# Mask-row copies and casts on more engines, with a new order of the work behind batch 0

## The chip, the cores and the metric

The kernel runs on one core of a Trainium2 chip. The core has engines that each execute their own queue of instructions in order: TensorE (PE, with the loading of its weights shown as PEld), VectorE (DVE), ScalarE (ACT), GpSimd (POOL) and SyncE (SP), which here only issues DMA transfers. An instruction whose input is not ready waits, and everything behind it in the same queue waits with it. The metric is the device time of one execution in microseconds (us); smaller is better.

## The reference

Sparse attention is followed by a two-layer network. There are 4 batches, 8 heads, 768 positions and 64 dimensions a head. The keys of a head form 12 blocks of 64. A query's gate scores are its products with the mean key of each block; blocks that lie wholly after the query's own are excluded. A query may attend to the three blocks with the largest scores and to its own block, causally.

```python
k_rep = k.reshape(B, H, n_blocks, block, D).mean(axis=3)
gate_scores = np.einsum('bhsd,bhnd->bhsn', q, k_rep)
gate_scores = np.where(causal, gate_scores, -1000000000.0)
top_idx = np.argsort(gate_scores, axis=-1)[..., -top_k:]
...
scores = np.where(mask, scale * q @ k.T, -1000000000.0)   # mask: chosen blocks and causal
attn_out = softmax(scores) @ v
x = attn_out.transpose(0, 2, 1, 3).reshape(3072, 512)
out = gelu_tanh(x @ w_in) @ w_out          # w_in 512x2048, w_out 2048x512
```

(The last lines are shortened; the softmax is that of each row.)

## The kernel before

**Units.** The heads of a batch are taken two at a time, which gives 16 pairs: pair p belongs to batch p // 4. In the texts, pair 6 is the third pair of batch 1. The network is computed batch by batch as soon as a batch's four pairs are done, so that attention of batch b + 1 runs beside the network of batch b on the same engines.

**Preparing a pair** (`pre(p)`). For pairs from 4 on, queries and keys are loaded by SP in blocks of 32 (line L400, four DMAs for each of q and k) and transposed on DVE (L564). DVE sums the key blocks (L621) and builds the gate's operand (L638). Casts to 16 bits put the transposed keys into `kT` (`kc_all`, one cast for each head) and the queries into `qT` (`q16`, one for each head). The gate is a group of small matmuls (L687). DVE transposes its result (L703), adds the causal part (L710), finds the largest values (L719, ten MAX8), compares (L720) and writes the additive mask `madd` (L724). The mask has 12 rows for each head, one for each key block, once it is turned: they become rows 64 to 76 of `qT`, so that one matmul over 76 rows gives score plus mask. For pairs 4 to 7 the turning is done on PE (L756) and the result lies in PSUM; for pairs 8 to 15 it is a DMA transpose issued by SP (L763) into a tile `mT` in SBUF. From there `mc` copies the 12x640 rows of each head into `qT`. All casts and copies whose engine can be chosen go through `copy` (L361 to L367): L363 is ACT, L365 POOL, L367 DVE.

**Heads** (`heads(p)`). Each head has three groups. A group is a set of score matmuls (L1046) into one of two "wide" PSUM buffers, the exponential on ACT (L1059), a causal select on POOL (L1073), and the matmuls with the values (L1085). DVE divides by the row sums (L968, L969), and the result is turned for the network, on PE (L988) or by a DMA transpose (L993).

**The network.** `s1` is x @ w_in (L1122) with gelu on ACT (L1134). For batch 0 the second product is plain (L1322). For batches 1 to 3 it is computed with seven products of half-size blocks in place of eight (L1372); DVE makes the sums of blocks that this needs (L1309) and joins the results (L1421), and `a_e` copies one part. Batch 3 uses the same trick for the first product (`s1_seven`: L1211, DVE additions at L1170). Filler matmuls (L1524), whose results are not used, stand at some places of PE's queue.

**What sets the order.** The program first records 1,900-odd operations, each with the engines that it may run on and an estimated cost for each. The order of issue, the choice of buffers and the engines were found by a planner beforehand and stand in the file as three tables: `ORDER` (L21, operation numbers), `BUFFER` (L157, buffer picks in that order) and `ENGINE` (L183, operations that don't run on the first engine of their list). `Plan.run` replays them:

```python
for n in ORDER:
    op = self.ops[n]
    for kind, key in op.takes:
        if key not in self.buf:
            self.buf[key] = self.kinds[kind][0][next(picks)]
    op.emit(engine.get(n, next(iter(op.engines))))
```

Each engine gets its operations in the sequence in which they stand in `ORDER`; semaphores between engines are placed by the framework. The cost figures in the calls of `add` are not used when the kernel runs: they are what the planner reckoned with, and their keys are the engines that it could choose.

Of the kernel before, what the change touches and what calls it, by code (L numbers as in the profile page):

```python
# [189 lines left out]
    "POOL": [  # L190
        586, 587, 646, 647, 707, 972, 973, 1035, 1036, 1097, 1098,
        1159, 1160, 1425, 1489, 1551, 1612]}


class Op:
# [40 lines left out]
def kernel(  # L236
# [121 lines left out]
    add = plan.add  # L358
# [169 lines left out]
    def pre(p):  # L528
# [238 lines left out]
        if first:  # L767
            mcs = []
# [858 lines left out]
```

## Time and profile before

| | us |
|---|---|
| median of 3 runs | 257.55 (257.46 to 257.74) |
| the profiled execution | 257.76 |
| span of its instructions | 256.0 |
| PE busy | 246.5 (96%) |
| DVE busy | 191.4 (75%) |
| ACT busy | 176.4 (69%) |
| POOL busy | 84.3 (33%) |
| mean clock that PE was granted | 1.0 of full speed |

The profiled execution is 1.76 us longer than the span, and 0.21 us above the median. Shares are those of the span. In the rows, "L1059 ACT ACTIVATE ats<-wide 128x896 x72 | 63.4, 915 | 8.9 <-PE" reads: line, engine, operation, output from input, shape, count; busy us in total and mean ns of one; idle us of the engine just before them and what ended most of it. A row of a timeline begins with the start and the duration in us, and ends, where the engine sat idle before, with the idle time and its releaser. A row of a table by stretch has for each engine its busy us (and its number of instructions), then the clock, the share of DMA and GB/s. `SPq` are DMA issues in SP's queue.

### The profile page before, as it was taken

How to read it: one execution, taken by the hardware profiler on the slowest of the kernel's cores; microseconds unless marked ns; L12 is line 12 of the kernel's file. 1: busy time of each engine (PE TensorE's matmuls, PEld its weight loads, DVE VectorE, ACT ScalarE, POOL GpSimd, SP SyncE). 2: the span in 40 equal slices, each digit the busy share in tenths (PEclk: the TensorE clock that was granted, in tenths of full speed). 3: DMA queues.
4: the chain of work that ended last, by engine and by line, in shares of the span. 5: the costliest groups of instructions: out<-in, count | busy, mean ns of one | idle time of the engine just before them, and what ended most of it. 6: DMA issues, size and time to landing. Idle time of an engine off the chain costs nothing.

```text
span 256.0 us, 6451 instructions
## 1 busy us (share of the span) xinstructions
PE 246.5 (96%) x2485; PEld 171.2 (67%) x2485; DVE 191.4 (75%) x539; ACT 176.4 (69%) x225; POOL 84.3 (33%) x163
## 2 busy tenths in 40 slices
PE   7889999999998999999899999999999999999994
PEld 5667686555554566555578888555777786766883
DVE  2769751041989889989999999699889665579954
ACT  2399997634898998667969884566889957557300
POOL 8465970000239366223053853100056620000000
PEclk9999999999999999999999999999999999999999
DMA  8997599999989995999899699532112520040024
GB/s 164 218 208 166 94 212 191 213 161 157 184 142 165 153 143 99 172 179 199 127 174 110 144 188 166 118 94 69 26 34 72 64 74 1 3 165 0 3 82 164
DMA packets 130927, 32.62 MB, mean 127 GB/s; under 512 B 124528, under 2 KB 126928, under 8 KB 130896
## 3 DMA queue, kind: packets, MB, share of 16 engines
q1 hardware_dynamic: 126160, 27.62, 65.4%
q0 software_dynamic: 3136, 4.19, 9.7%
q10 hardware_dynamic: 1600, 0.39, 0.8%
q8 instruction: 19, 0.31, 0.5%
q14 instruction: 12, 0.10, 0.1%
HBM read 27.26 MB, written 6.29 MB: 131 GB/s over the span
## 4 chain that ended last, share of the span: by engine, by line
PE 51%; DVE 16%; SPq 11%; DMA 10%; POOL 4%; issue 3%; ACT 3%; ACTq 1%; DVEq 0%; POOLq 0%
PE bank L1372 17%; PE wide L1122 10%; SPq L400 9%; PE wide L1046 6%; PE wide L1211 5%; DMA w_in<-in_moe_w_in_dram 5%; PE bank L1085 5%; PE bank L1322 3%; DVE qT L367 3%; DMA sd<-in_k_dram 3%; DVE sel L719 2%; DVE s L564 2%; DVE XS L1309 2%; DMA G<-in_q_dram 2%; ACT ats L882 1%
## 5 line engine op out<-in xcount | busy, mean ns | idle before, releaser
L1122 PE MATMUL wide<-xT,w_in 128*128 128x384 f16 x416 | 72.6, 326 | 0.0
L1059 ACT ACTIVATE ats<-wide 128x896 f16<-128x896 f32 x72 | 63.4, 915 | 8.9 <-PE wide L1046 6.2
L1134 ACT ACTIVATE G<-wide 128x768 f16<-128x768 f32 x52 | 42.1, 810 | 27.3 <-PE wide L1122 27.0
L1122 PEld LDWEIGHTS <-w_in 128*128 128x128 f16 x416 | 40.0, 98 | 26.8 <-issue 1.3
L1073 POOL TENSOR_SCALAR_AFFINE_SELECT ats<-ats 128x256 f16<-128x256 f16 x72 | 33.3, 475 | 60.3 <-ACT ats L1059 60.2
L1046 PE MATMUL wide<-qT,kT 76*128 76x512 f16 (+3 forms) x192 | 39.1, 305 | 0.1
L564 DVE STREAM_TRANSPOSE s<-sd 128x768 f32<-128x768 f32 x24 | 23.1, 968 | 18.7 <-DMA sd<-in_k_dram 17.2
L1372 PE MATMUL bank<-w_out,G 128*128 128x256 f16 x216 | 31.4, 272 | 0.0
L1372 PEld LDWEIGHTS <-G 128*128 128x128 f16 x288 | 26.9, 98 | 6.0 <-issue 0.3
L1322 PE MATMUL bank<-w_out,G 128*128 128x512 f16 x96 | 28.1, 379 | 0.0
L365 POOL CAST kT<-s 64x768 f16<-64x768 f32 x17 | 15.2, 891 | 37.5 <-DVE s L564 37.0
L1421 DVE TENSOR_TENSOR osb<-bank,osb 128x512 f32<-128x512 f32 (+1 forms) x38 | 22.1, 592 | 5.1 <-PE bank L1372 4.5
L1085 PEld LDWEIGHTS <-ats 128*128 128x128 f16 x504 | 22.2, 98 | 3.9 <-POOL ats L1073 0.4
L1085 PE MATMUL bank<-v,ats 128*128 128x65 f16 x504 | 24.4, 194 | 0.2 <-POOL ats L1073 0.2
L1046 PEld LDWEIGHTS <-kT 76*128 76x128 f16 x192 | 17.3, 98 | 10.5 <-issue 0.8
L1372 PEld LDWEIGHTS <-XS 128*128 128x128 f16 x216 | 20.0, 98 | 5.5 <-DVE XS L1309 1.5
L1372 PE MATMUL bank<-TS,XS 128*128 128x256 f16 x144 | 22.0, 272 | 0.8 <-DVE XS L1309 0.7
L882 ACT ACTIVATE ats<-wide 128x1024 f16<-128x1024 f32 (+3 forms) x24 | 20.8, 924 | 1.3 <-PE wide L863 0.8
L365 POOL CAST v<-vsd 128x768 f16<-128x768 f32 x13 | 11.4, 875 | 13.8 <-DMA vsd<-in_v_dram 8.8
L969 DVE TENSOR_TENSOR xn<-bank,zr 128x384 f16<-128x384 f32 x24 | 13.4, 558 | 0.8
L719 DVE MAX8 sel<-sel 128x8 f32<-128x12 f32 x160 | 13.2, 158 | 0.6
L1322 PEld LDWEIGHTS <-G 128*128 128x128 f16 x96 | 8.9, 98 | 6.1 <-issue 0.3
(120 smaller groups left out, 358.6 us busy)
## 6 DMA issues: line engine op xcount, KB each, us to landing
out_dram<-osb SPq DMA_DIRECT2D x23, 256.0 KB
vsd<-in_v_dram SPq DMA_DIRECT2D x26, 192.0 KB
sd<-in_k_dram SPq DMA_DIRECT2D x48, 96.0 KB
sd<-in_q_dram SPq DMA_DIRECT2D x48, 96.0 KB
w_in<-in_moe_w_in_dram POOLq DMA_DIRECT2D x2, 1024.0 KB, 11.5
w_out<-in_moe_w_out_dram POOLq DMA_DIRECT2D x2, 1024.0 KB, 14.5
G<-in_k_dram SPq DMA_DIRECT2D x4, 192.0 KB
G<-in_q_dram SPq DMA_DIRECT2D x4, 192.0 KB
```

The source lines that it names most:

```text
L365: nc.gpsimd.tensor_copy(out=out, in_=in_)
L400: nc.sync.dma_start(out=T[key, p][64 * hh + 32 * a:64 * hh + 32 * a + 32], in_=SRC[key][b, 2 * hp + hh].rearrange("(t i) (a j) -> a i t j" ...
L564: nc.vector.transpose(out=T[key + "T32", p], in_=T[key, p].rearrange("p t j -> p (t j)"))
L882: nc.scalar.activation(out=T["at", u][:, :, 0:n], in_=plan.buf[("st",) + u].rearrange("p (h w) -> p h w", h=2)[:, :, 0:n], func=AF.Exp, bi ...
L1046: nc.tensor.matmul(st[:, x:e], kT16[i][h][0:76, s0:s0 + 128], qT16[i][h][0:76, s0 + (x - cb):s0 + (e - cb)], start=True, stop=True)
L1059: nc.scalar.activation(out=T["at", u][:, 0:n], in_=plan.buf[("st",) + u][:, 0:n], func=AF.Exp, bias=0.0, scale=SCALE)
L1073: nc.gpsimd.affine_select(out=dg, in_=dg, compare_op=ALU.is_ge, fill=0.0, base=0, pattern=[[0, 2], [1, 128]], channel_multiplier=-1)
L1085: nc.tensor.matmul(pvv[:, qc, 0:65], at[:, cb + (qc - jc) * 128: cb + (qc - jc + 1) * 128], v16[i][:, jc, h, :], start=(gi == 0 and jc == ...
L1122: nc.tensor.matmul(hps[:, 512 * e:512 * e + HALF], w_in16[:, ci, (2 * j + e) * 128: (2 * j + e + 1) * 128], T["xT", b][:, ci, HALF * h:HAL ...
L1134: nc.scalar.activation(out=G[:, :, h, j, :], in_=plan.buf["hps", b, j, h].rearrange("p (e w) -> p e w", e=2)[:, :, 0:HALF], func=AF.Gelu_a ...
L1322: nc.tensor.matmul(plan.buf["ops", b, ti], G[:, f % 2, 2 * ti // NC, f // 2, ti % (NC // 2) * 128:ti % (NC // 2) * 128 + 128], w_out16[:, ...
L1372: nc.tensor.matmul(dst[:, HD * h:HD * h + HD], FACT[m][0][:, j, t * 128:(t + 1) * 128], FACT[m][1][:, j, :], start=(clear and j == 0), sto ...
```

## The change

Four entries of the planner's tables are widened or revised, and the three recorded tables are replaced by the ones that a further search gave.

```diff
-            kcs = [add({DVE: 0.56, POOL: 0.85}, kc_all(h),
+            kcs = [add({DVE: 0.56, POOL: 0.85, ACT: 0.84}, kc_all(h),
...
-            q16s = [add({DVE: 0.56, ACT: 0.84}, q16(h), qcs + [old.get("s")],
+            q16s = [add({DVE: 0.56, ACT: 0.84, POOL: 0.85}, q16(h), qcs + [old.get("s")],
...
-                m = add({"DMA": 0.8}, lambda _: None, [go], pr, lag=6.0)
+                m = add({"DMA": 0.8}, lambda _: None, [go], pr, lag=3.5)
...
-            mcs = [add({DVE: 0.5, ACT: 0.7} if byPE else {DVE: 0.33}, mc(h),
+            mcs = [add({DVE: 0.5, ACT: 0.7} if byPE else
+                       {DVE: 0.4, POOL: 0.72, ACT: 0.66}, mc(h),
...
 ENGINE = {
     "ACT": [
         67, 72, 74, 85, 90, 94, 101, 110, 114, 121, 130, 134, 141,
-        329, 331, 345, 346, 348, 449, 467, 486, 504, 523, 541, 580,
-        595, 597, 628, 657, 658, 718, 893, 929, 980, 981, 1043, 1044,
-        1106, 1167, 1202, 1434, 1559, 1668, 1674, 1677, 1698, 1704,
-        1707, 1727, 1736, 1786, 1822],
+        329, 331, 348, 349, 449, 467, 486, 504, 523, 541, 580, 587,
+        597, 598, 628, 657, 857, 893, 929, 972, 973, 985, 1035, 1036,
+        1047, 1048, 1167, 1172, 1202, 1425, 1438, 1489, 1550, 1668,
+        1674, 1677, 1698, 1704, 1707, 1727, 1733, 1736, 1786, 1822],
     "POOL": [
-        586, 587, 646, 647, 707, 972, 973, 1035, 1036, 1097, 1098,
-        1159, 1160, 1425, 1489, 1551, 1612]}
+        345, 346, 586, 646, 647, 655, 707, 708, 716, 984, 1097, 1098,
+        1106, 1159, 1160, 1168, 1171, 1426, 1437, 1496, 1500, 1501,
+        1551, 1562, 1563, 1612, 1613, 1624, 1625]}
```

The mask-row copies from `mT` could only run on DVE before and may run on three engines now. The first 346 entries of `ORDER`, with all of batch 0's attention, are the same. Behind them `ORDER` and `BUFFER` differ throughout (some 100 lines of numbers, left out here). Eight filler matmuls (operations 1921 to 1928) are no longer in `ORDER`: three stood near 63 us of the profiled execution, one near 70 us, and four between 230 and 235 us.

Forty-five operations run on another engine:

| from, to | what |
|---|---|
| DVE to ACT (10) | mask rows from PSUM of pairs 4 and 5 (349, 598); mask rows from `mT` of pairs 8, 9, 11 and 12 (985, 1047, 1048, 1172, 1438); a key cast of pair 14 (1550); one `a_e` copy (857) and one copy of 128x768 in `s1_seven` (1733) |
| DVE to POOL (16) | mask rows from `mT` of pairs 8 and 11 to 15 (984, 1171, 1437, 1500, 1501, 1562, 1563, 1624, 1625); seven casts of pairs 6, 7, 11, 12, 13 and 15 (655, 708, 716, 1168, 1426, 1496, 1613) |
| ACT to DVE (9) | mask rows from PSUM of pairs 6 and 7 (658, 718); seven query casts of pairs 5, 8, 9, 12 and 14 (595, 980, 981, 1043, 1044, 1434, 1559) |
| ACT to POOL (3) | query casts of pairs 4 and 10 (345, 346, 1106) |
| POOL to ACT (7) | key casts of pairs 5, 8, 9, 12 and 13 (587, 972, 973, 1035, 1036, 1425, 1489) |

Among the other moves in `ORDER`, the gates of pairs 14 and 15 stand some 6 us of PE work earlier, and SP's DMA issues from pair 12 on stand in another sequence. What is computed is the same.

255 rows, old and new, of tables (BUFFER, ORDER) are left out of this document.

## The prediction

> **What bounds the kernel now.** I read the page's busy line and chain first, then TensorE's waits, then its idle time by stretch, and last the other engines there.
>
> ```profile
> PE 246.5 (96%) x2485; PEld 171.2 (67%) x2485; DVE 191.4 (75%) x539; ACT 176.4 (69%) x225; POOL 84.3 (33%) x163
> PE 51%; DVE 16%; SPq 11%; DMA 10%; POOL 4%; issue 3%; ACT 3%; ACTq 1%; DVEq 0%; POOLq 0%
> ...
> PE bank L756 <- DVE madd L724: 1.2, 1, 1.2
> PE bank L1372 <- DVE XS L1309: 0.7, 1, 0.7
> PE bank L1085 <- POOL ats L1073: 0.2, 1, 0.2
> ```
>
> TensorE (PE) is busy for 246.5 of 256.0 us, so other engines count only where they make it wait. The last three rows are its waits from 61 us on, where the two orders part (columns: us, times, longest). The same shows by stretch:
>
> ```profile
> core 0: us, PE busy (x) PEld busy (x) DVE busy (x) ACT busy (x) POOL busy (x), PEclk, DMA share, GB/s
> 75.00:85.00 10.00, 8.80 (x91) 5.24 (x88) 9.68 (x27) 8.77 (x12) 8.58 (x15) 1.00 1.06 161
> 85.00:97.00 12.00, 11.96 (x149) 7.33 (x147) 10.38 (x32) 10.71 (x15) 5.78 (x12) 1.00 0.92 126
> 97.00:110.00 13.00, 13.00 (x131) 8.07 (x129) 12.53 (x43) 10.25 (x13) 4.87 (x7) 1.00 1.04 145
> 122.00:135.00 13.00, 12.07 (x121) 8.88 (x119) 12.69 (x46) 10.08 (x14) 4.18 (x8) 1.00 1.13 147
> 185.00:205.00 20.00, 19.76 (x252) 15.34 (x250) 16.25 (x33) 17.89 (x21) 13.16 (x25) 1.00 0.32 54
> ...
> 61.00:140.00 79.00, 76.84 (x720) 47.62 (x719) 70.85 (x206) 63.01 (x81) 31.91 (x53) 1.00 1.07 156
> 140.00:205.00 65.00, 64.76 (x698) 47.74 (x696) 56.85 (x153) 49.94 (x62) 24.85 (x46) 1.00 0.56 96
> ```
>
> Between 61 and 205 us PE lacks 79.00 − 76.84 + 65.00 − 64.76 = 2.4 us. Half of it lies at 75 to 85 (1.20) and most of the rest at 122 to 135 (0.93), in both of which VectorE (DVE) is full: 9.68 of 10 and 12.69 of 13 us. Of DVE's slack, then, the change can sell at most about 2.4 us of PE time. ACT at 17.89 of 20 in the last heads, and DVE at 12.53 of 13 at 97 to 110, are full without costing PE anything: they are where a new wait would come from.
>
> **The change, part by part.** The first 346 entries of the order are the same, to about 61 us; so what is lost before that stays.
>
> *Fillers.* Eight filler matmuls (L1524) go: three near 63 us, one near 70, four between 230 and 235.
>
> ```profile
> 230.43 0.38 PE L1372 MATMUL bank<-w_out,G 128*128 128x256 f16 x2
> 230.65 0.27 PE L1524 MATMUL bank<-XS 128*128 128x256 f16 x1
> 230.76 0.81 PE L1211 MATMUL wide<-sd 128*128 128x384 f16 x4
> ```
>
> From a filler's start to the next matmul's is 0.11 us, so eight hold 0.88. No wait stands beside them; if they only filled time in which PE would have waited, they return 0. I take −0.7, nearer to the rows.
>
> *Who does the copies.* Forty-five copies and casts change engine: from DVE ten go to ACT and sixteen to GpSimd (POOL); ACT gives nine to DVE and three to POOL; POOL gives seven key casts to ACT. Their prices:
>
> ```profile
> L367 DVE COPY qT<-mT 12x640 f16<-12x640 f16 x16 | 7.1, 445 | 0.4
> L367 DVE CAST qT<-s 64x768 f16<-64x768 f32 x13 | 8.6, 660 | 0.2
> L363 ACT CAST qT<-s 64x768 f16<-64x768 f32 x11 | 9.1, 827 | 0.2
> L363 ACT COPY qT<-bank 12x640 f16<-12x640 f16 x5 | 3.4, 680 | 1.8 <-PE bank L756 0.9 <-DVE qT L367 0.8
> L365 POOL CAST kT<-s 64x768 f16<-64x768 f32 x17 | 15.2, 891 | 37.5 <-DVE s L564 37.0
> L510 POOL MEMSET madd<- 128x640 f16 x4 | 2.6, 644 | 0.0
> L367 DVE COPY qT<-bank 12x640 f16<-12x640 f16 x3 | 1.5, 488 | 0.7 <-ACT qT L363 0.7
> L367 DVE COPY osb<-bank 128x256 f32<-128x256 f32 x5 | 2.1, 419 | 2.6 <-PE bank L1372 2.6
> L367 DVE COPY ats<-wide 128x768 f32<-128x768 f32 x1 | 1.0, 958 | 0.1
> L363 ACT COPY ats<-wide 128x768 f32<-128x768 f32 x5 | 4.0, 799 | 3.1 <-PE wide L1211 3.1
> L1059 ACT ACTIVATE ats<-wide 128x896 f16<-128x896 f32 x72 | 63.4, 915 | 8.9 <-PE wide L1046 6.2
> ```
>
> DVE loses fourteen of its sixteen copies of turned mask rows (14 × 0.445 = 6.2), eight casts (8 × 0.66 = 5.3) and two evictions (0.42 + 0.96), and takes seven casts (4.6): about −8.3 us. ACT takes eight casts (6.6), five mask copies (5 × 0.68 = 3.4) and the two evictions (0.80, and some 0.4 for the smaller), and gives ten casts (8.3): about +2.9, two PSUM mask copies each way cancelling. POOL takes nine mask copies and ten casts and gives seven casts: 3 × 0.89 + 9 × a price the trace does not show. A copy of 12x640 lies between 0.445 (DVE's row) and 0.89 (POOL's larger cast); I take 0.65, the MEMSET with the same 640 columns: 5.9, so +8.5. None of this is on the path by itself; what counts is the wait that it ends or makes.
>
> *The wait at 81.74.*
>
> ```profile
> 76.79 1.78 DVE L367 CAST qT<-s 64x768 f16<-64x768 f32 x2
> ...
> 79.37 0.82 DVE L719 MAX8 sel<-sel 128x8 f32<-128x12 f32 x10
> 80.22 1.06 DVE L720 TENSOR_TENSOR sel<-sel,sel 128x120 f32<-128x120 f32 x1
> ...
> 81.74 0.45 PE L756 MATMUL bank<-ident,madd 128*128 128x128 f16 x5 [1.20 <-DVE madd L724]
> ```
>
> PE waits 1.20 us for pair 6's selection. Ahead of it in DVE's queue two mask copies from PSUM now go to ACT (2 × 0.49, DVE's price for that form) and one of the two casts at 76.79 to POOL (half of 1.78); one cast comes in (0.66). That is 0.98 + 0.89 − 0.66 = 1.2 us earlier, with the mask matmul at its old place in PE's order. Between 0 (POOL's cast stands in DVE's way) and −1.2, I take −1.0.
>
> *The wait at 126.71.* Here DVE does two selections in a row and then the sums (L1309) that the halves at L1372 need. In the new order the four copies of turned mask rows of pairs 8 and 9 leave DVE (1.8 us), against one cast more (0.66): the sums come about 1.1 us earlier, more than the 0.72 that PE waited. I take −0.7, and 0 as the other end. The 0.2 behind the selects (L1073) goes with the new order of the last heads: −0.2 to 0, taken −0.2.
>
> *What is late next: ACT.* Behind each moved copy on ACT stand exps of 0.915 us, and PE's second matmuls (L1085) stand behind those through POOL's select. From 85 to 97 ACT has 10.71 of 12 us; in the new order about one mask copy or cast of 0.7 to 0.83 more stands there, and from 117 to 130 the three copies on ACT wait for a DMA transpose first. I put 0 to 0.8 on each place; by the durations the first is the likelier to be late: +0.5 and +0.3.
>
> *What is late next: DVE at 97 to 122.* Two query casts of pairs 8 and 9 come from ACT into the stretch that begins with 12.53 of 13 us, 2 × 0.66 = 1.3 us, ahead of transposes, selections and the gate of pair 11. The work in DVE's queue from pair 9's query transpose to that gate, each instruction by its duration in this trace, sums to 18.8 to 19.7 us, and the new order has 18.8 us of PE work beside it: 0 to +1.0, taken +0.3.
>
> *The gates of pairs 14 and 15, moved.* They stood here:
>
> ```profile
> 166.96 0.94 DVE L564 STREAM_TRANSPOSE s<-sd 128x768 f32<-128x768 f32 x1
> ...
> 153.61 1.64 SPq L993 DMA_TRANSPOSE xT<-xn  x1
> 158.36 4.08 SPq L400 DMA_DIRECT2D sd<-in_q_dram  x4
> 167.80 0.75 PE L687 MATMUL bank<-s,ksb 128*32 128x160 f32 x16
> ```
>
> The same pair of gates now comes some 6 us of PE work earlier, and PE executes in order: whatever is behind them waits too. Pair 15's query load (four DMAs, 4.08 us of SP's queue) stands behind the DMA transposes of the outputs of pairs 8, 9 and 10 (the last issued at 153.61), as before, and DVE's transpose (0.94) behind the load. In SP's new queue its key load and the value load of pair 13 are ahead of these transposes (3.0 us) and others behind (some 2.9), so that the load comes only 1 to 3 us earlier; its transpose then ends at 164 to 167 less the slack of 2 to 4 us that DVE had ahead of it, 162 to 164, and PE comes to the gates at about 163: 0 to +1.0, taken +0.3.
>
> *The mask copies in ACT's and POOL's queues.* Now an in-order queue with exps or selects behind waits for a DMA transpose.
>
> ```profile
> L763 SPq DMA_TRANSPOSE mT<-madd x8: 1200/1238/2685, 106.6 to 182.8; - x8
> L367 DVE COPY qT<-mT x16: 317/319/939, 120.0 to 193.1; 12x640 f16<-12x640 f16 x16
> ```
>
> The first copy started 13.4 us after the first issue and the last ones 10.3 us after the last, so the rows do not show how short the lag may be; if it is below the planner's new 3.5 plus 0.8, no copy of the new order comes early by my walk through it. 0 to +1.5 for the worst single hold; taken +0.1, near the lower end, since the rows' lags are long. Sundry small waits of a new order that I can't place: +0.2.
>
> *Sum* against the profiled execution, 257.76 us (span 256.0 and 1.76 around it): −0.7 − 1.0 − 0.7 − 0.2 + 0.5 + 0.3 + 0.3 + 0.3 + 0.1 + 0.2 = −0.9. The additions are taken at a third to two thirds of their upper ends, since the walk found little slack there but no certain wait. The profiled execution stands 0.21 above the median of 257.55, so that the median of the changed kernel is put at 257.55 − 0.9 = 256.65, rounded 256.6.
>
> **A page's rule against it.** In the rows above, the compare at 80.22 (L720) took 1.06 us; the one at 72.43 took 0.28.
>
> ```profile
> 72.43 0.28 DVE L720 TENSOR_TENSOR sel<-sel,sel 128x120 f32<-128x120 f32 x1
> 80.33 0.82 POOL L365 CAST v<-vsd 128x768 f16<-128x768 f32 x1
> ```
>
> A POOL cast of 0.82 ran over it, and the excess is 0.78: DVE stood still for it. The Trainium skill, "SBUF — State Buffer", section "Who interferes with whom", says that a DVE instruction with two SBUF inputs, or a copy or cast in a two-port mode, and a GpSimd instruction that reads SBUF share one port pair, an exclusive lock: the second fully blocks until the first ends. The trace agrees with it in this row. By that rule each of the 19 operations that POOL takes could hold DVE for its whole length, where a sum without it lets both run side by side (−0.9); what that would come to is the first rival.
>
> **Rivals.**
> *POOL holds DVE (slower).* Place: the query cast of pair 6 and two casts of pair 7 on POOL between 77 and 97 us, a mask copy at 120 to 122. For: the row at 80.22, and a full DVE there. Against: POOL takes what DVE no longer does, and from 160 to 185 PE works on long matmuls without need of DVE. Price: the 1.0 at 81.74 isn't gained, and three locks of 0.78 (2.3) reach PE: −0.9 + 1.0 + 2.3 = +2.4, 259.9. It decides from two locks that reach PE on (1.6 against the gain of 0.9).
> *A queue held by a mask copy (slower).* ACT or POOL waits for the DMA transpose with three exps behind: one hold of 1.5 and the gates' 1.0 in place of the taken 0.1 and 0.3: −0.9 + 1.4 + 0.7 = +1.2, 258.8. It decides from a hold of about 1.0 on. For: 14 of 16 such copies leave DVE; against: 10 to 13 us of lag in the rows.
> *It does nothing that can be measured.* PE's waits only move: fillers return 0.4, and what the ended waits give the new ones take: 257.0 to 258.0, with 257.2 by these numbers. The three runs spread over 0.28 us, so 0.2% (0.5 us) is about what a measurement of this kernel can tell from no change.
> *Nearly all waits go.* −0.88 for the fillers, −2.1 for the three waits, and none new: 254.6, the floor, since PE's own work is unchanged.
>
> **How the numbers follow.** Forecast (255.5 to 257.0) 0.40; nearly all gone 0.10; nothing measurable 0.14; POOL holds DVE 0.20; a queue held 0.16. So faster 0.50, same 0.14, slower 0.36. The range leaves out half of the floor case and about a tenth above: 255.0 to 260.8; the likeliest case alone has 255.5 to 257.0. An order with so many hands changed has small waits that no walk by hand finds, and that is why slower keeps more than a third.
>
> **What would show it.** Right: PE's wait of 1.2 us for the selection at L724 is gone, that of 0.7 for L1309 too, PE busy near 245.7, idle from 61 to 205 us near 1.5, DVE busy down by 5 to 9 us, POOL up by some 8. Wrong: a wait of PE for L703 or L564 at the moved gates, for L1059 or L1073 at the second matmuls, compares and casts on DVE of 0.8 us or more beside POOL's new copies, or copies of `mT` on ACT or POOL that end a long idle time of their engine with a DMA named as the cause. The prediction falls if PE's idle time from 61 to 205 us is over 2.9 us, which uses up what the fillers give.

## The result, and the profile after

The changed kernel takes 260.91 us (260.81 to 261.02, 4 runs) where the kernel before takes 257.61 us beside it: a ratio of 1.0128, with a 95% interval of 1.0111 to 1.0146. It is 3.3 us slower. The profiled execution has a span of 259.1 us, 3.1 more than before. First the page's busy line of the changed kernel, then its waits of PE from 61 us on (us, times, longest), then PE's table by stretch.

```profile
PE 246.5 (95%) x2477; PEld 171.0 (66%) x2477; DVE 186.5 (72%) x522; ACT 179.5 (69%) x230; POOL 93.6 (36%) x175
...
PE bank L1086 <- POOL ats L1074: 1.9, 2, 1.6
PE wide L1123 <- DMA xT<-xn: 1.8, 1, 1.8
PE wide L1047 <- ACT ats L1060: 1.1, 1, 1.1
PE bank L756 <- DVE madd L724: 0.7, 2, 0.4
PE bank L687 <- DVE s L564: 0.7, 1, 0.7
...
61.00:140.00 79.00, 77.20 (x734) 48.37 (x733) 69.96 (x203) 65.03 (x84) 31.71 (x55) 1.00 0.97 151
140.00:205.00 65.00, 60.82 (x643) 44.29 (x641) 51.08 (x135) 48.62 (x60) 29.85 (x51) 1.00 0.61 101
```

(Line numbers behind about 800 are one higher than before; in the experiments' rows they are three or four lower, since their tables are set in fewer lines.) ACT has 3.1 us more and POOL 9.3 more, about as reckoned (2.9 and 8.5); DVE has only 4.9 less, where 8.3 were reckoned. From 61 to 140 us PE's idle time fell from 2.16 to 1.80 us. From 140 to 205 us, where it had been 0.24, it is now 65.00 − 60.82 = 4.18. So the loss was made in a part of the kernel that had none to lose, and three waits carry it: for the outputs' DMA transpose (1.8), at the moved gates (0.7) and for a causal select (1.6). In the earlier stretch the waits at 81.74 and 126.71 are gone, and three others, of 1.06, 0.39 and 0.34 us, stand there.

### The profile page after: what moved, and what is told of

Same layout as the page of the kernel before. It is cut to its first block, busy times and chain, and to the rows that moved or that the text cites. A ratio compares the mean times of both kernels' runs of the same rounds, so it can differ in the third digit from the quotient of the medians.

```text
span 259.1 us, 6443 instructions
## 1 busy us (share of the span) xinstructions
PE 246.5 (95%) x2477; PEld 171.0 (66%) x2477; DVE 186.5 (72%) x522; ACT 179.5 (69%) x230; POOL 93.6 (36%) x175
## 4 chain that ended last, share of the span: by engine, by line
PE 73%; DVE 9%; ACT 6%; POOL 4%; DMA 3%; issue 2%; SPq 2%; DVEq 0%; POOLq 0%; ACTq 0%
PE wide L1123 24%; PE bank L1373 16%; PE wide L1047 7%; PE bank L1323 6%; PE wide L1212 5%; PE bank L1086 5%; ACT ats L1060 2%; PE wide L864 2%; PE bank L932 2%; POOL ats L1074 2%; PE bank L1525 2%; PE bank L687 2%; ACT ats L883 2%; DMA sd<-in_q_dram 1%; SPq L400 1%
## 5 line engine op out<-in xcount | busy, mean ns | idle before, releaser
L1123 PE MATMUL wide<-xT,w_in 128*128 128x384 f16 x416 | 73.4, 326 | 1.9 <-DMA xT<-xn 1.8
L1135 ACT ACTIVATE G<-wide 128x768 f16<-128x768 f32 x52 | 42.1, 811 | 28.6 <-PE wide L1123 28.0
L1074 POOL TENSOR_SCALAR_AFFINE_SELECT ats<-ats 128x256 f16<-128x256 f16 x72 | 32.0, 458 | 50.1 <-ACT ats L1060 49.3
L1373 PE MATMUL bank<-w_out,G 128*128 128x256 f16 x216 | 33.9, 272 | 0.0
L1373 PEld LDWEIGHTS <-G 128*128 128x128 f16 x288 | 26.9, 98 | 6.0 <-issue 0.3
L1373 PE MATMUL bank<-TS,XS 128*128 128x256 f16 x144 | 22.8, 272 | 0.1
L365 POOL CAST qT<-s 64x768 f16<-64x768 f32 x7 | 6.4, 922 | 21.3 <-DVE ksb L638 21.0
L365 POOL COPY qT<-mT 12x640 f16<-12x640 f16 x9 | 7.8, 871 | 14.4 <-DMA mT<-madd 14.0
```

The source lines that it names most:

```text
L365: nc.gpsimd.tensor_copy(out=out, in_=in_)
L1074: nc.gpsimd.affine_select(out=dg, in_=dg, compare_op=ALU.is_ge, fill=0.0, base=0, pattern=[[0, 2], [1, 128]], channel_multiplier=-1)
L1123: nc.tensor.matmul(hps[:, 512 * e:512 * e + HALF], w_in16[:, ci, (2 * j + e) * 128: (2 * j + e + 1) * 128], T["xT", b][:, ci, HALF * h:HAL ...
L1135: nc.scalar.activation(out=G[:, :, h, j, :], in_=plan.buf["hps", b, j, h].rearrange("p (e w) -> p e w", e=2)[:, :, 0:HALF], func=AF.Gelu_a ...
L1373: nc.tensor.matmul(dst[:, HD * h:HD * h + HD], FACT[m][0][:, j, t * 128:(t + 1) * 128], FACT[m][1][:, j, :], start=(clear and j == 0), sto ...
```

## The experiments

**Four mask copies back on DVE.** The wait of 1.6 us for a select lies at 192 us, in the last heads. POOL's timeline of the changed kernel there (start, us):

```profile
186.75 0.92 POOL L365 COPY qT<-mT 12x640 f16<-12x640 f16 x1
187.72 1.05 POOL L365 CAST kT<-s 64x768 f16<-64x768 f32 x1
188.84 0.61 POOL L1074 TENSOR_SCALAR_AFFINE_SELECT ats<-ats 128x256 f16<-128x256 f16 x1
189.51 1.32 POOL L365 COPY qT<-mT 12x640 f16<-12x640 f16 x1
190.90 1.28 POOL L1074 TENSOR_SCALAR_AFFINE_SELECT ats<-ats 128x256 f16<-128x256 f16 x2
...
192.24 0.61 PE L1086 MATMUL bank<-v,ats 128*128 128x65 f16 x14 [1.58 <-POOL ats L1074]
```

POOL works here without a pause, and two mask copies stand between the selects. The first experiment moves only the engines:

```diff
 # ENGINE["POOL"] of the changed kernel: mask copies of pairs 14 and 15
-        1551, 1562, 1563, 1612, 1613, 1624, 1625
+        1551, 1612, 1613
```

> The changed kernel with only the four turned-mask copies of pairs 14 and 15 back on DVE (from POOL); order as changed. Theory A (POOL's queue): these copies, 0.8 to 1.3 us each on POOL, stand between the causal selects of the last heads, and PE's 1.6 us wait for a select at 192 us comes from them; the wait falls below 0.4 and the time by 1.2 to 1.7 us, to 259.2 to 259.7. Theory B (the new order is tight everywhere): the wait moves to exps or selects next to it, gain under 0.5, 260.4 or more.

Measured: 260.09 us, ratio to the kernel before 1.0095 (1.0082 to 1.0108), which is 0.8 us better than the changed kernel and lies between the times of the two theories. The wait is gone as theory A has it, but not all of its time came back:

```profile
PE wide L1119 <- DMA xT<-xn: 2.5, 2, 1.7
PE bank L1082 <- POOL ats L1070: 0.3, 1, 0.3
```

PE's waits for a select fell from 1.9 to 0.3; in this execution those for `xT`, which lie ahead of the edit, were longer by 0.7. Since PE's order is that of the changed kernel, the start of the same matmul can be compared in the two traces: PE is 0.6 us later than there at 159.47, 1.2 earlier behind the select (192.24), and 0.7 earlier from 195.4 on, behind a new wait for a normalization on DVE. So the copies on POOL made that wait; the gain in time, 0.8, is below the 1.2 that was expected.

**One key load behind a DMA transpose.** The wait for `xT` is a wait for DMA transposes which SP issues. SP's timeline of the changed kernel:

```profile
151.60 1.26 SPq L994 DMA_TRANSPOSE xT<-xn  x1
152.92 1.71 SPq L400 DMA_DIRECT2D sd<-in_k_dram  x3
154.74 1.21 SPq L994 DMA_TRANSPOSE xT<-xn  x1
156.04 2.20 SPq L394 DMA_DIRECT2D vsd<-in_v_dram  x2
158.29 4.45 SPq L400 DMA_DIRECT2D sd<-in_q_dram  x7
...
159.47 0.48 PE L1123 MATMUL wide<-xT,w_in 128*128 128x384 f16 x2 [1.84 <-DMA xT<-xn]
```

Three DMAs of pair 15's key load go out at 152.92, and the transpose of pair 10's output only behind them.

```diff
 # ORDER, SP's operations only
-    1597, 1015, 918, 1077, 1598, 1139, 1543, 1544, 1540, 1601, 1602
+    1597, 1015, 918, 1077, 1139, 1598, 1543, 1544, 1540, 1601, 1602
```

> The changed kernel with one entry of the order moved: the last three DMAs of pair 15's key load are issued behind the DMA transpose of pair 10's output instead of ahead of it in SP's queue. Theory A (SP's queue): the transpose is issued some 1.7 us earlier, PE's wait of 1.8 us for xT at 159 us falls to 0 to 0.4, time 259.0 to 259.6. Theory B: the transpose lands late because the DMA engines are shared with the loads, or the pair 15 gate becomes late by the same amount; gain under 0.6, 260.3 or more.

Measured: 260.78 us, ratio 1.0135 (1.0112 to 1.0158): no gain. Four of the six runs lie at 260.39 to 260.88, the other two at 262.14 and 262.26. PE's wait for `xT` in this run, and the gates of pairs 14 and 15, first in the changed kernel and then here:

```profile
PE wide L1119 <- DMA xT<-xn: 0.5, 1, 0.5
...
167.15 0.75 PE L687 MATMUL bank<-s,ksb 128*32 128x160 f32 x16 [0.66 <-DVE s L564]
...
166.75 0.75 PE L683 MATMUL bank<-s,ksb 128*32 128x160 f32 x16 [1.92 <-DVE s L560]
```

The wait at 159.47 is gone, as theory A has it (the 0.5 that is left belongs to another transpose, at 154.75), and the wait at the gates rose from 0.7 to 1.9, so that the outcome is that of theory B. But the gates did not become later: they start 0.4 us earlier than in the changed kernel. The query loads are issued 0.3 us later than there (158.56 against 158.29), which is next to nothing, and PE simply comes sooner to gates that wait for them. The wait for `xT` had covered most of this second wait.

**The rest of SP's queue.** The value load of pair 14, whose matmuls come some 30 us later, stood ahead of the query loads of pairs 14 and 15. It is moved behind them, and the whole key load of pair 15 behind the transpose.

```diff
 # ORDER, SP's operations only
-    1597, 1015, 918, 1077, 1598, 1139, 1543, 1544, 1540, 1601, 1602
+    1015, 918, 1077, 1139, 1597, 1598, 1540, 1601, 1602, 1543, 1544
```

> The changed kernel with only SP's queue re-sequenced between 145 and 163 us: all four DMAs of pair 15's key load behind the DMA transpose of pair 10's output, and the value load of pair 14 behind the query loads of pairs 14 and 15. Theory A (what stands ahead in SP's queue makes both waits): PE's wait for xT (1.8 us) and its wait at the moved gates (0.7 us; 1.9 us where only the key load was moved) are both below 0.4; time 258.3 to 259.1. Theory B (the DMA engines are the limit, so one of the two is late whatever the sequence): the sum of both stays above 1.5 us, 260.1 or more.

Measured: 258.63 us, ratio 1.0037 (1.0024 to 1.0050). The time is that of theory A, 2.3 us less than the changed kernel, but by waits it is only half right. No wait for `xT` is left. The wait at the gates, which theory A had below 0.4, is longer than in the changed kernel, 1.5 against 0.7, and the sum of both stands at the bound that theory B gave. Some 1.0 of the gain comes from waits for a select, which fell from 1.9 to 0.9 without an edit there; the second mask copy took 0.92 us on POOL here and not 1.32, and what made it shorter was not tested.

```profile
164.75 0.98 DVE L560 STREAM_TRANSPOSE s<-sd 128x768 f32<-128x768 f32 x1 [0.80 <-DMA sd<-in_q_dram]
...
165.78 0.48 PE L683 MATMUL bank<-s,ksb 128*32 128x160 f32 x8 [1.49 <-DVE s L560]
```

DVE itself waits for the query load, and PE for DVE: DVE's second query transpose starts 1.4 us earlier than in the changed kernel (166.11), but PE, without the wait ahead, is there 2.2 us earlier. These gates come too soon for loads in any of the three sequences.

**Two copies of one PSUM tile.** The wait of 1.06 us at 85 us is for an exp. ACT and DVE in the changed kernel:

```profile
82.89 0.49 DVE L367 COPY qT<-bank 12x640 f16<-12x640 f16 x1
...
81.13 0.92 ACT L1060 ACTIVATE ats<-wide 128x896 f16<-128x896 f32 x1 [0.32 <-PE wide L1047]
83.42 0.68 ACT L363 COPY qT<-bank 12x640 f16<-12x640 f16 x1 [1.36 <-DVE qT L367]
84.12 2.54 ACT L1060 ACTIVATE ats<-wide 128x896 f16<-128x896 f32 x3
...
85.09 0.54 PE L1047 MATMUL wide<-qT,kT 76*128 76x512 f16 x3 [1.06 <-ACT ats L1060]
```

The two heads' mask rows of pair 6 lie in one PSUM tile. The change gave one copy to DVE, whose copy stands behind normalizations and a transpose, and ACT's copy, later in `ORDER`, waits for it with the exps behind.

```diff
 # ORDER: ACT's copy (657) and DVE's copy (658)
-    658, 609, ..., 657
+    657, 658, 609, ...
```

> The changed kernel with the two PSUM mask copies of pair 6 in the other sequence: ACT's copy (head 0) is issued ahead of DVE's (head 1). Engines unchanged. Theory A (two readers of one PSUM tile on two engines are put in program order): ACT's wait of 1.36 us on DVE's copy goes, and PE's wait of 1.06 us for an exp at 85 us falls below 0.3; time 259.8 to 260.3. Theory B: ACT was waiting for something else, or PE's wait is made by the exps' own sum; no gain, 260.6 or more.

The mechanism was right: no wait of PE at 85 us and none of ACT on DVE's copy is left in the trace, and PE reaches the next gate 1.2 us sooner. The time was not what was expected: 261.09 us median, with single runs at 259.39 and 259.89 and four from 260.88 to 261.76 (ratio 1.0122, 1.0093 to 1.0151). The same stretch of the changed kernel and of this run's profiled execution (260.88 us) shows what happened (the seventh figure is the granted clock):

```profile
190.00:195.00 5.00, 3.42 (x49) 2.52 (x47) 4.03 (x8) 3.10 (x4) 3.81 (x6) 1.00 0.02 5
...
190.00:195.00 5.00, 4.31 (x37) 3.02 (x38) 3.20 (x6) 1.59 (x3) 2.32 (x4) 0.66 0.14 52
```

Behind the wait for the select, which this kernel still has, PE was granted a clock of 0.66 in the mean over 5 us, and 0.50 in each whole microsecond from 191 to 194. That is 0.34 × 5 = 1.7 us of PE work lost, more than the gain of 1.2: PE's lead over the changed kernel, 1.6 us at 159.47, is used up between 192.5 and 194.1. The runs themselves bear it out: the two short ones have a mean clock of 1.0 over the whole execution, and the four long ones 0.993, a loss of 1.8 us in 259. (The two long runs of the experiment on the key load have 0.993 as well.) The two short ones average 259.64 us, 1.3 less than the changed kernel: where the clock holds, the edit gives what was expected. What decides whether it holds is not shown.

**The fillers alone.** The eight fillers were taken out of the kernel before, with their entries in `BUFFER`.

```diff
 # ORDER of the kernel before
-    454, 1921, 1922, 1923, 342, ...
+    454, 342, ...          # and the same for 1924 to 1928
```

> The kernel before without the eight filler matmuls behind 61 us, all else as before. By the prediction's term: 0.7 us less, 256.8 to 257.0. Rival: the fillers only fill time in which PE would wait anyway, so 257.3 to 257.7; or they keep something in step and the time grows.

Measured: 257.45 us, ratio 0.9989 (0.9980 to 0.9997): 0.3 us, not 0.7. PE near 63 us, first in the kernel before and then here, and last here in the tail:

```profile
62.98 0.49 PE L1524 MATMUL bank<-XS 128*128 128x256 f16 x3
63.40 0.48 PE L687 MATMUL bank<-s,ksb 128*32 128x160 f32 x8
...
62.76 0.38 PE L1318 MATMUL bank<-w_out,G 128*128 128x512 f16 x1
63.07 0.48 PE L683 MATMUL bank<-s,ksb 128*32 128x160 f32 x8
...
230.14 0.38 PE L1368 MATMUL bank<-w_out,G 128*128 128x256 f16 x2
230.47 0.81 PE L1207 MATMUL wide<-sd 128*128 128x384 f16 x4
```

Without the three fillers near 63 us the gate comes 0.33 us sooner (63.07 against 63.40). In the tail nothing more is gained. Where a filler stood between 230.43 and 230.76 in the kernel before, the same two matmuls are again 0.33 us apart (230.14 and 230.47), now with a gap between them, and the lead is 0.29 us at the first of the four fillers and 0.31 behind the last (234.43 against 234.74). These four stood in time in which PE would have waited in any case.

**Three of the engine moves alone.** In the kernel before, with its order unchanged, the mask copies of pairs 4 and 5 (one head each) go to ACT and one query cast of pair 6 to POOL.

```diff
 # ENGINE of the kernel before
-    "ACT": [..., 348, ..., 597, ...], "POOL": [..., 647, 707, ...]
+    "ACT": [..., 348, 349, ..., 597, 598, ...], "POOL": [..., 647, 655, 707, ...]
```

> The kernel before, order unchanged, with three of the engine moves only: the mask copies of pairs 4 and 5 (head 1) from DVE to ACT and one query cast of pair 6 from DVE to POOL. By the prediction's term for the wait at 81.74: that wait of 1.2 us falls below 0.4, time 256.6 to 257.1. Rival (ACT's 1.4 us more makes exps late in a stretch where ACT has 9.6 of 10 us): a new wait of PE for exps of the same size, 257.5 or more.

Measured: 256.69 us, ratio 0.9961 (0.9947 to 0.9975), 1.0 us faster. That is the time which was expected, but it did not come from this wait:

```profile
81.65 0.45 PE L753 MATMUL bank<-ident,madd 128*128 128x128 f16 x5 [0.48 <-DVE madd L721]
...
80.44 1.15 DVE L721 SCALAR_TENSOR_TENSOR madd<-sel,ownm 128x120 f16<-128x120 f32 x1
```

The wait fell from 1.2 to 0.5, but the mask matmul behind it starts only 0.09 us sooner than in the kernel before (81.74). PE's order is the same in both, and their traces run together to 0.05 us up to 76 us. Then ACT's eviction and exps behind the added copies start 0.6 us later (76.80 against 76.19, 77.28 against 76.68), PE, which needs them, falls 0.6 us behind, and the selection's wait is shorter because PE comes later to it. The 1.0 came further on, with the order unchanged: PE is 0.09 us ahead up to 119, 0.25 at 120, 0.75 behind the sums that it waited for at 126.71, and 0.94 from 134 on.

DVE's relief bore little fruit as well. With the three gone it sat idle for 1.68 us until the gate's result came from PE, and began the selection at 78.06 in place of 78.60: 0.54 us sooner and not 1.2. Two steps of the selection were then long: L707 took 0.77 us beside the very cast that was moved to POOL (78.25 to 79.07), and the last step, L721, 1.15 us beside a cast and a select on POOL (80.23 to 81.45), where 0.28 is usual for both. Each ended 0.14 us after POOL did. Most of the rest of the relief went into these slower steps; that POOL is the cause is argued from these times and was not tested alone.

**Nine mask copies on POOL alone.** The counterpart: the kernel before with the nine copies from `mT` on POOL that the change puts there.

```diff
 # ENGINE["POOL"] of the kernel before
-        ..., 707, 972, ..., 1489, 1551, 1612
+        ..., 707, 972, 984, ..., 1171, ..., 1437, 1489, 1500, 1501, 1551, 1562, 1563, 1612, 1624, 1625
```

> The kernel before, order and all else unchanged, with the nine copies of turned mask rows on POOL that the change puts there. Theory A (POOL's copies of 0.7 to 1.3 us hold the selects whatever the order): PE gets a new wait for a select near 192 to 196 us and the time is 258.3 to 259.5. Rival (they hurt only in the new order, where they stand between selects that PE wants at once): within 0.3 of the kernel before, 257.4 to 258.0.

Measured: 263.28 us, ratio 1.0222 (1.0206 to 1.0238): 5.6 us slower, more than either theory gave.

```profile
196.28 2.09 POOL L362 COPY qT<-mT 12x640 f16<-12x640 f16 x2
...
197.66 0.90 PE L1043 MATMUL wide<-qT,kT 76*128 76x512 f16 x3 [3.39 <-POOL qT L362]
...
195.00:200.00 5.00, 2.35 (x15) 1.27 (x15) 2.00 (x3) 0.92 (x1) 4.31 (x7) 0.64 0.00 0
200.00:205.00 5.00, 5.00 (x46) 3.71 (x45) 0.70 (x3) 3.04 (x4) 1.99 (x4) 0.67 0.00 0
```

In this order PE's score matmuls wait for the copies themselves, 3.4 us, and the granted clock then drops to 0.64 and 0.67 in two stretches of 5 us; each of the five runs has a mean clock of 0.986 to 0.992. The change's new order softened what its move to POOL costs; it did not remove it.

**All edits together.** The four copies on DVE, pair 6's copies in the other sequence and SP's queue as above, on the changed kernel.

> All the edits tried on the changed kernel together: four mask copies on DVE, pair 6's copies in the other sequence, SP's queue as in the run beside this. Theory A (the loss is a few local waits): gains add up, 0.8 + 1.2 + 2.2 off 260.9, 256.2 to 257.2, at or below the kernel before. Theory B (a tight order in which waits only move): 257.8 or more.

Measured: 257.05 us, ratio 0.9977 (0.9964 to 0.9990), 0.2% faster than the kernel before. The single gains of 0.8 and 2.3, with 1.2 for the wait at 85 us, make 4.3; 3.9 of them came, and no wait at 85 us or for `xT` is left. Theory A holds: the loss was a few local waits. In a last step three matmul groups were moved later in PE's queue:

```diff
 # ORDER: gates of pairs 14, 15 and DVE's transpose; mask matmuls of pairs 5 and 7
-    1616, 1617, 1555, 1432, 1556, 1494, ..., 1262
+    1616, 1432, 1494, ..., 1262, 1617, 1555, 1556
-    596, 490, 491, 569, 645, 492, 493          -    717, 519
+    490, 491, 569, 645, 492, 493, 596          +    519, 717
```

> The run with all four edits, and three matmul groups moved later in PE's queue: the gates of pairs 14 and 15 (with DVE's transpose of the first) by 1.6 us of PE work, the mask matmuls of pair 5 by 1.1 us, those of pair 7 by 0.2 us. Theory A (each of these waits is PE coming too early to one group): the waits at the gates (0.6) and for pair 5's mask (0.3) go, 0.8 to 1.2 us off: 255.7 to 256.4, faster than the kernel before. Theory B (DVE's chain is late for all that follows as well): less than 0.4 off.

Measured: 255.90 us, ratio 0.9933 (0.9920 to 0.9945). This is 0.7% faster than the kernel before and 5.0 us faster than the changed one, and the time is that of theory A. Of the waits, those for the masks fell (L752, from 1.1 to 0.3), while 0.6 at the gates is left, now in two parts. No wait of PE behind 61 us is longer than 0.3 us:

```profile
PE bank L683 <- DVE s L560: 0.6, 2, 0.3
PE bank L752 <- DVE madd L720: 0.3, 1, 0.3
PE bank L1082 <- POOL ats L1070: 0.3, 1, 0.3
```

## Why the prediction was wrong

It put 256.6 us, with 255.0 to 260.8 and even odds of a gain; the result is 260.91.

- *Where the time goes first.* The gains were sought and found where PE waited: the wait at 81.74 and that at 126.71 are gone. The first was priced at −1.0 from three engine moves; alone they brought its matmul only 0.09 us sooner, because DVE then waited for the gate, and two of its steps took longer beside POOL. Their 1.0 us came further on, half of it at the second, so that the agreement with the price is luck. Which other move ended the first wait in the changed kernel was not tested. The loss is elsewhere: PE's idle time from 61 to 205 us, which the prediction would not have above 2.9, rose from 2.4 to 6.0 (1.80 + 4.18). That is 3.6 more, and with the 0.3 that the fillers gave it makes the 3.3 us.
- *The fillers*, −0.7, were mis-sized: 0.3 measured, from those near 63 us. For the four in the tail the other price, 0, was right: they fill waiting time. Absence of a wait beside a filler showed nothing, because the filler itself had covered it.
- *The mask copies in POOL's queue*, +0.1, is the first step that failed. It looked for a copy that waits for its DMA and took 0.65 us for one on POOL. The trace after has this:

```profile
L365 POOL COPY qT<-mT x9: 709/802/1322, 119.4 to 198.5; 12x640 f16<-12x640 f16 x9
```

  None waited for its DMA in the last heads; they simply occupied POOL for 0.92 to 1.32 us each between selects that PE wanted at once. That made 1.6 us of wait, which went with the copies. The rival "a queue held by a mask copy" named the queue, but gave it the DMA as cause. Waits of POOL for such a DMA are in the trace (14.0 us in two, the sign that the prediction named), but they end at 119.4 and 174.6, where PE has no wait.
- *The DMA transposes of the outputs* are the second, and no term stood for them at all. The prediction saw that pair 15's key load had come ahead of these transposes in SP's queue, and priced only what stands behind them, the query load and the gates. The transposes themselves were thereby late for batch 2's first product: 1.8 us at 159.47, which went when the key load was issued behind the transpose.
- *The gates of pairs 14 and 15*, +0.3 in a range of 0 to 1.0: the mechanism was right and the size too small. It cost 0.7 only because the wait for `xT` stands ahead of it; where that wait is gone, it is 1.5 to 1.9, above the upper end, and taking that wait away alone gave no time.
- *ACT at 85 to 97*, +0.5: 1.06 came, at 85 us, but not from the sum of ACT's work. It came from one copy's wait for another on DVE. *ACT at 117 to 130* and *DVE at 97 to 122*, +0.3 each, cost nothing: PE is busy throughout from 97 to 135.
- *POOL holds DVE*, the first rival, is there; by PE's waits it has about a third of its price. Two of the waits that stand are for selections in which an instruction took about three times its usual 0.28 us beside a POOL cast:

```profile
73.65 0.79 DVE L724 SCALAR_TENSOR_TENSOR madd<-sel,ownm 128x120 f16<-128x120 f32 x1
88.84 0.90 DVE L710 TENSOR_TENSOR sel<-sel,cgate 128x120 f32<-128x120 f32 x1
...
73.44 0.86 POOL L365 CAST v<-vsd 128x768 f16<-128x768 f32 x1
88.77 0.81 POOL L365 CAST kT<-s 64x768 f16<-64x768 f32 x1
...
74.49 0.45 PE L756 MATMUL bank<-ident,madd 128*128 128x128 f16 x5 [0.34 <-DVE madd L724]
91.37 0.45 PE L756 MATMUL bank<-ident,madd 128*128 128x128 f16 x5 [0.39 <-DVE madd L724]
```

  Both instructions have two inputs in SBUF; they ended 0.14 and 0.16 us after the cast did. The Trainium skill, "SBUF — State Buffer", section "Who interferes with whom", says that the one of such a pair that issues second blocks fully until the first ends; the two rows agree with it, for in both the cast started first. (In the row of the kernel before at 80.22 the compare starts ahead of the cast, at 80.33, but a POOL select was already running from 79.97 to 80.37: the hold there took in two POOL instructions, not the cast alone.) The two waits come to 0.7 us. It was not tested by taking the casts away. DVE's busy time shows more of it, first in the kernel before and then in the changed one:

```profile
L710 DVE TENSOR_TENSOR sel<-sel,cgate 128x120 f32<-128x120 f32 x15 | 4.2, 281 | 0.3
L1309 DVE TENSOR_TENSOR G<-G 128x768 f16<-128x768 f16 x12 | 6.9, 578 | 0.1
...
L710 DVE TENSOR_TENSOR sel<-sel,cgate 128x120 f32<-128x120 f32 x15 | 5.8, 385 | 0.3
L1310 DVE TENSOR_TENSOR G<-G 128x768 f16<-128x768 f16 x12 | 8.8, 765 | 0.0
```

  The copies and casts that moved came to 9.5 us less on DVE by their rows, a little more than the 8.3 that were reckoned. But its steps with two inputs at L710, L720, L724 and L1310 together took 46.7 us in place of 42.1, so that DVE was relieved of 4.9 us in all. In the trace after, each of these steps that took over one and a half times its usual time ran beside an instruction on POOL. The prediction priced what leaves DVE and not what this makes of the rest.

The sum was therefore made of the right kinds of terms, but it counted one queue's moves only for the instruction that was moved, and not for each one that it was put ahead of.

## What to carry to other kernels

When a new order is judged, walk each in-order queue, the DMA issuer's among them, and ask for every operation that is put earlier what now stands behind it and who waits for that. A stretch in which the busiest engine had no wait deserves as much care as those with waits, for there only losses can arise. An operation's price on another engine must come from that engine next to the work that it will run beside: the copies of 0.32 us on DVE were 0.71 at best on POOL, and 0.92 to 1.32 among the selects. And a wait that gets shorter is not yet a gain, nor is one that gets longer a loss, for the engine may have come later or sooner to it: compare when the same instruction starts in the two traces. At the gates the wait grew from 0.7 to 1.9 while they started 0.4 us earlier; at the selection near 81.7 it fell by 0.7 for a gain of 0.09.

## What was not expected of the hardware

A single wait of PE cost more than its length. Behind a wait of 1.58 us the granted clock was 0.50 for some 3.4 us (0.90, three times 0.50 and 0.89 in five rows of 1 us) in one execution, and behind one of 3.39 us it was 0.64 and 0.67 over 10 us; behind the same wait of 1.58 us in the profiled execution of the changed kernel it stayed at 1.00. The Trainium skill, "TensorE: Matmul & The Clock Gate", section 'Part 1: The HAM clock gate (the "warmup" mystery)', puts the gate at half rate after an idle window of about 3.4 us and says that the window runs freely; the half rate and the change from execution to execution agree, while here a wait of 1.58 us was enough.

Two copies that read one PSUM tile on two engines followed one another in program order: ACT waited 1.36 us for DVE's, and no longer once it was issued first. The Trainium skill, "PSUM — Partial Sum Buffer", section "PSUM bank collisions raise a hardware error", says that two engines may not access the same bank in the same quadrant of 32 partitions at a time, reads with reads included, and that different quadrants of one bank are free of this. The two copies read rows 0 to 11 and 64 to 75 of the tile (`src[64 * h:64 * h + 12, :]`), which are different quadrants, so by that section they need not have followed one another. The order is that of the program, kept by its semaphores, and no run let both read at once.
